# Attention with mixed heads and a token/channel MLP: another order in the last double steps and the tail

## The chip, the cores and the metric

The kernel runs on one core of one Trainium2 chip. The metric is the device time of one execution in microseconds (us), the median of the runs; it begins and ends a little outside the span from the first to the last instruction that the profile shows.

## The reference

```python
def _attn_ref(q, k, v, w_pre, w_post):          # q, k, v: (4, 12, 448, 64)
    scores = scale * np.matmul(q, k.transpose(0, 1, 3, 2))
    scores = np.einsum('bhij,hg->bgij', scores, w_pre)      # mixes the 12 heads
    scores = scores - np.max(scores, axis=-1, keepdims=True)
    attn = np.exp(scores)
    attn = attn / (np.sum(attn, axis=-1, keepdims=True) + 1e-09)
    attn = np.einsum('bhij,hg->bgij', attn, w_post)         # mixes them again
    return np.matmul(attn, v)

def _moe_ref(x, w_tok1, w_tok2, w_ch1, w_ch2):  # x: (4, 448, 768), the heads side by side
    h = np.maximum(x.transpose(0, 2, 1) @ w_tok1, 0.0) @ w_tok2
    u = x + h.transpose(0, 2, 1)
    return u + np.maximum(u @ w_ch1, 0.0) @ w_ch2
```

The four MLP weights arrive as 64-bit floats; the kernel converts each into a pair of single-precision parts, a high one and a remainder.

## The kernel before, in words

The attention part cuts each batch's 448 rows into four tiles (T = 0 to 15 over the batches), and each tile into groups of ten rows. One or two groups make a step (92 of them), two steps a double step J (46, from J = 0 to 45, with two more to fill the pipe). The order of all work is written out by hand; each engine takes its instructions in that order, and a planner at the start hands the score products (`qk`) and value products (`av`) of the tiles to the double steps. From J = 40 on there are no score products left, and each double step has one value product, of tile 13 (J = 40 to 42) or 14 (J = 43 to 45). Tile 15's three come behind the loop. "av(14,1)" is tile 14's second value product.

A step passes through three double steps. In the first (steps `na` and `nb`), `pre` mixes heads on TensorE (L169), `mx` takes two row maxima on VectorE (L177), `ex` takes the exponentials on ScalarE (L186), the first half at once for `na`. In the second (`ea`, `eb`), the rest of the exponentials follow, `rec` forms sums and reciprocals on VectorE (L195, L198), and GpSimd normalises (L200, L203). In the third (`pa`, `pb`), `post` mixes heads again on TensorE (L212) and `turn` transposes 32x32 blocks on VectorE (L225). `av` multiplies with v (L242); ScalarE copies one half of its result (L254), VectorE adds the other ("the sum", L256), and a DMA stores it (L257).

PSUM has two pools in this part. `pre` has two tiles. Another pair is shared by post, av and the score products, in turn: in J = 43 to 45 each of them needs the tile of the one before the last, and so waits for that one's `turn` or sum.

`cv_tick` moves the conversion of the weights on by one position i: a DMA loads unit i+5 (L356), ScalarE writes the high part of unit i (L377), VectorE assembles unit i+1 in three operations (L386, L390, L396), another engine forms the remainder of unit i (L394), GpSimd clamps magnitudes of unit i+2 (`cv_clamp`, L368), and ScalarE takes magnitudes of unit i+3 (`cv_abs`, L362). Units 0 to 7 are the token weights (128x256 four times, 128x224 four times), the others the channel weights. It is called 2, 1, 1, 3 times in the last four double steps, and 4 times among tile 15's value products.

`load_x` brings a batch's x back from DRAM (L345; batches 0 and 1 at the beginning of J = 43 and 44). `tr(b, hfs)` transposes halves of it on TensorE (L513: four PSUM tiles of three transpositions per half), ScalarE writes high parts (L518), VectorE remainders (L520). Then, for each batch, `tok1` and `tok2` multiply with the token weights (L528 to L530, L542, L543), with `tr` of the next batch in between; `tok2` also forms u (L559) and, for batch 0, its high part (L563) and remainder (`u_lo`, L580). `ch1` and `ch2` (from 442 us to the end) multiply with the channel weights. The tail before was in this order:

```python
    av(NT - 1, 0)
    tr(0, (0,))
    cv_tick(1)
    av(NT - 1, 1)
    tr(0, (1,))
    cv_tick(1)
    av(NT - 1, 2)
    cv_tick(2)
```

Of the kernel before, what the change touches and what calls it, by code (L numbers as in the profile page):

```python
# [14 lines left out]
ALU = mybir.AluOpType  # L15
AX = mybir.AxisListType
PSUM = bass.MemoryType.PSUM
# [19 lines left out]
def attn_mixer_kernel(  # L37
# [12 lines left out]
    nc = tc.nc  # L50
    f32 = lambda ap: ap.bitcast(F32)
# [11 lines left out]
    def en(name, **kw):  # L63
        p = tc.alloc_tile_pool(name=name, reuse_waits="tile", **kw)
        opens[name] = p
        return p

    def close(*names):
        for n in names:
            opens.pop(n).release()  # L70
# [233 lines left out]
    G = 0  # L304
# [60 lines left out]
    def cv_clamp(i):  # L365
        P = units[i][1]
        g = mags[i]
        nc.gpsimd.tensor_scalar(  # L368
            out=g[:P], in0=g[:P], scalar1=MAG_MIN, scalar2=MAG_MAX, op0=ALU.max, op1=ALU.min,
        )  # L370

# [79 lines left out]
    def step(i):  # L451
        return steps[i] if 0 <= i < NS else []

    for J in range(-2, ND):
        pa, pb, ea, eb, na, nb = [step(2 * J + i) for i in range(6)]
        if J == ND - 4:
            close("early")
            open_prep()
        if J == ND - 1:
            close("ps")  # L460
            a2 = en("a2", bufs=2, side="right")
            pst = en("pst", bufs=4, space=PSUM, side="right")
        for fn, *a in loads[J]:
            fn(*a)
        if J in (ND - 3, ND - 2):
            load_x(J - ND + 3)
        for st in (pa, pb):
            if st:
                post(st)
        if ea:  # L470
            ex(ea, 1)
        if pa:
            turn(pa)
        if ea:
            rec(ea)
            ex(eb, 0)
            ex(eb, 1)
        if pb:
            turn(pb)
        if eb:  # L480
            rec(eb)
        if J >= ND - 4:
            cv_tick((2, 1, 1, 3)[J - ND])
        if na:
            pre(na)
            mx(na)
        for a in value[J][:1]:
            av(*a)
        for a in score[J][:1]:
            qk(*a)  # L490
        if nb:
            pre(nb)
            ex(na, 0)
        for a in value[J][1:]:
            av(*a)
        for a in score[J][1:]:
            qk(*a)
        if nb:
            mx(nb)
        for st in (step(2 * J + 8), step(2 * J + 9)):  # L500
            for G in st:
                regroup(G)

    XN, H1 = {}, {}

    def tr(b, hfs=(0, 1)):
        x = XR[b]
        xn = XN.get(b) or [a2.tile([128, JT - i, DM], F32R, tag=f"xn{i}", bufs=1, name=f"xn{i}") for i in range(2)]
        for hf in hfs:
            for j in range(JT):  # L510
                p = pst.tile([128, 512], F32, tag="tr", name="tr")
                for d in range(3):
                    nc.tensor.transpose(  # L513
                        out=p[:, 128 * d:128 * d + 128], in_=x[hf][:, d, min(128 * j, 320):min(128 * j, 320) + 128],
                        identity=prep["ident"],
                    )
                cs = slice(384 * hf, 384 * hf + 384)
                nc.scalar.copy(out=xn[0][:, j, cs], in_=p[:, :384])  # L518
                lo_t, r = (xn[1][:, j, cs], 0) if j < 3 else (xn[0][:64, 3, cs], 64)
                nc.vector.tensor_tensor(out=lo_t, in0=p[r:, :384], in1=f32(xn[0])[r:, j, cs], op=ALU.subtract)  # L520
        XN[b] = xn

    def relu_split(p, h, l):
        nc.scalar.activation(out=h, in_=p, func=ACTF.Relu)  # L524
# [7 lines left out]
    def tok1(b):  # L532
        xn = XN.pop(b)
        h1 = [a3.tile([128, 2, DM], F32R, tag=f"h1{i}", bufs=1, name=f"h1{i}") for i in range(2)]
        for hf in range(2):
            for m in range(2):
                p = psa.tile([128, 512], F32, tag="t", bufs=4, name="pt1")
                cs = slice(384 * hf, 384 * hf + 384)
                w = [y[:, :, 128 * m:128 * m + 128] for y in prep["t1"]]
                for j in range(3):  # L540
                    mm3(p[:, :384], [y[:, j] for y in w], [y[:, j, cs] for y in xn], j == 0, False)
                nc.tensor.matmul(out=p[:, :384], lhsT=w[0][:, 3], rhs=xn[0][:, 3, cs], start=False, stop=False)  # L542
                nc.tensor.matmul(out=p[:, :384], lhsT=w[1][64:, 3], rhs=xn[0][64:, 3, cs], start=False, stop=True)  # L543
                relu_split(p[:, :384], h1[0][:, m, cs], h1[1][:, m, cs])
                if hf * 2 + m < 2:
                    cv_tick(1)
        H1[b] = h1

# [28 lines left out]
        return U[b, d][0]  # L577

    def u_lo(b, d, u):
        nc.vector.tensor_tensor(out=U[b, d][1], in0=u, in1=f32(U[b, d][0]), op=ALU.subtract)  # L580

    av(NT - 1, 0)
    tr(0, (0,))
    cv_tick(1)
    av(NT - 1, 1)
    tr(0, (1,))
    cv_tick(1)
    av(NT - 1, 2)
    cv_tick(2)
    close("mid", "late", "atp", "ps_w")  # L590
    psa = en("psa", bufs=2, space=PSUM)
    prep["w"] = en("wres", bufs=1)
# [101 lines left out]
```

## Time and profile before

| | us |
|---|---|
| median of 3 runs (797.56 to 800.02) | 798.28 |
| the profiled execution | 798.18 |
| its span, first to last instruction | 796.1 |
| TensorE busy (matmuls) | 765.5 |
| VectorE busy | 462.3 |
| ScalarE busy | 334.1 |
| GpSimd busy | 305.3 |

PE is TensorE's matmuls, PEld its weight loads, DVE is VectorE, ACT ScalarE, POOL GpSimd, SP the SyncE queue that issues the DMAs. Busy shares are means over stages with different limits; idle time of an engine matters where another waits for it. In the timelines a row has the start, the busy time, engine, line, operation, output and input, and in brackets the idle time of the engine ahead of it with what ended it.

### The profile page before, as it was taken

Reading aid. Unit: us, or ns where it says so; the run is one execution under the profiler, and the core shown is the slowest. Engines: PE = TensorE matmul, PEld = TensorE weight load, DVE = VectorE, ACT = ScalarE, POOL = GpSimd, SP = SyncE. Lnnn points to the kernel's source line nnn. Section 1 sums busy time; section 2 is a strip of 40 time slices with the busy share of each in tenths; the row PEclk is TensorE's granted clock in tenths of the full one; section 3 lists DMA queues with packets and bytes.
Section 4 is the critical chain, followed back from the end, with each engine's and each line's share of the span. In section 5 each row is a group of like instructions: output and inputs, shape, how many; then the busy total and the mean of one; then the engine's idle time right before and its main releaser. Section 6 shows DMA issues by size and latency. Waiting matters only on the chain.

```text
span 796.1 us, 21930 instructions
## 1 busy us (share of the span) xinstructions
PE 765.5 (96%) x9211; PEld 578.4 (73%) x9211; DVE 462.3 (58%) x822; ACT 334.1 (42%) x757; POOL 305.3 (38%) x292
## 2 busy tenths in 40 slices
PE   7879999999999999979999999999999999999998
PEld 3336555555555545557888999999999999999997
DVE  5766677777777677889899999950003100040002
ACT  3655766677766666556544355420001000020000
POOL 3663566555665465675267867600000000000000
PEclk9998999999999999999999999999999999999999
DMA  5784647755775474574565755351000300010001
GB/s 169 224 205 152 160 162 235 215 139 179 234 216 138 158 223 148 142 244 132 178 239 172 225 169 169 119 208 70 0 1 19 121 1 0 1 70 1 0 1 70
DMA packets 62594, 105.66 MB, mean 133 GB/s; under 512 B 20979, under 2 KB 49184, under 8 KB 61984
## 3 DMA queue, kind: packets, MB, share of 16 engines
q1 hardware_dynamic: 62080, 103.35, 42.1%
q8 instruction: 73, 1.20, 0.6%
q10 hardware_dynamic: 320, 0.87, 0.4%
q14 instruction: 25, 0.20, 0.1%
q0 software_dynamic: 96, 0.03, 0.0%
HBM read 49.18 MB, written 16.52 MB: 83 GB/s over the span
## 4 chain that ended last, share of the span: by engine, by line
PE 82%; DMA 7%; DVE 3%; ACT 2%; POOL 2%; issue 2%; SPq 1%; DVEq 0%; POOLq 0%; ACTq 0%
PE post L212 9%; PE pre L169 8%; PE av L242 7%; PE pc L528 7%; PE pc L529 7%; PE pc L530 7%; PE po L528 7%; PE po L530 7%; PE po L529 7%; PE qk L141 7%; DMA r<-s 4%; PE pt L528 2%; PE pt L530 2%; PE pt L529 2%; POOL e L203 1%
## 5 line engine op out<-in xcount | busy, mean ns | idle before, releaser
L203 POOL TENSOR_TENSOR e<-e,sm 128x896 f32<-128x896 f32 (+1 forms) x92 | 154.7, 1681 | 7.2
L525 DVE SCALAR_TENSOR_TENSOR rl<-pc,rh 128x448 fp32r<-128x448 f32 x48 | 29.8, 621 | 218.1 <-ACT rh L524 218.1
L225 DVE STREAM_TRANSPOSE at<-post 128x1024 f32<-128x1024 f32 (+1 forms) x92 | 111.9, 1216 | 40.7 <-PE post L212 40.6
L524 ACT ACTIVATE rh<-pc 128x448 fp32r<-128x448 f32 x48 | 26.1, 543 | 232.4 <-PE pc L530 232.3
L186 ACT ACTIVATE e<-pre,sm 128x448 f32<-128x448 f32 (+1 forms) x184 | 115.2, 636 | 8.3 <-DVE sm L177 8.0
L177 DVE TENSOR_REDUCE sm<-pre 128x2 f32<-128x896 f32 (+1 forms) x92 | 99.3, 1081 | 21.7 <-PE pre L169 21.3
L212 PE MATMUL post<-e,kpost 64*32 64x256 f32 x2880 | 99.3, 381 | 11.5 <-POOL e L203 4.4
L169 PE MATMUL pre<-r,kpre 64*64 64x448 f32 (+1 forms) x720 | 101.1, 554 | 7.5 <-DMA r<-s 4.4
L530 PE MATMUL pc<-u,w 128*128 128x448 f32 x288 | 105.2, 365 | 0.0
L529 PE MATMUL po<-rl,w 128*128 128x448 f32 x288 | 105.2, 365 | 0.0
L529 PE MATMUL pc<-u,w 128*128 128x448 f32 x288 | 105.2, 365 | 0.0
L528 PE MATMUL po<-rh,w 128*128 128x448 f32 x288 | 105.2, 365 | 0.0
L528 PE MATMUL pc<-u,w 128*128 128x448 f32 x288 | 105.2, 365 | 0.0
L530 PE MATMUL po<-rh,w 128*128 128x448 f32 x288 | 105.2, 365 | 0.0
L212 PEld LDWEIGHTS post<-e,kpost 64*32 64x32 f32 x2880 | 49.5, 106 | 70.8 <-issue 38.6
L141 PE MATMUL qk<-k,q 64*64 64x448 f32 (+2 forms) x768 | 97.7, 547 | 1.1 <-DMA k<-in_k_dram 0.5
L242 PEld LDWEIGHTS av<-at,v 64*64 64x64 f32 x2688 | 78.6, 136 | 23.3 <-DVE sm L195 9.8
L368 POOL TENSOR_SCALAR cv_g<-cv_g 128x384 f32<-128x384 f32 (+2 forms) x56 | 87.1, 1558 | 18.3 <-ACT cv_g L362 18.3
L200 POOL TENSOR_TENSOR e<-e,sm 128x128 f32<-128x128 f32 (+1 forms) x92 | 36.9, 401 | 143.2 <-ACT e L186 86.6
L242 PE MATMUL av<-at,v 64*64 64x120 f32 (+1 forms) x2688 | 84.3, 267 | 2.6 <-DVE x L256 2.5
L148 ACT COPY s<-qk 120x896 f32<-120x896 f32 (+1 forms) x84 | 75.5, 907 | 17.4 <-PE qk L141 11.1
L169 PEld LDWEIGHTS pre<-r,kpre 64*64 64x64 f32 (+1 forms) x720 | 33.3, 133 | 44.2 <-issue 31.9
(72 smaller groups left out, 1005.3 us busy)
## 6 DMA issues: line engine op xcount, KB each, us to landing
r<-s SPq DMA_DIRECT2D x176, 210.0 KB
cv_r<-in_w_ch_dram SPq DMA_DIRECT2D x48, 384.0 KB
v<-in_v_dram SPq DMA_DIRECT2D x16, 384.0 KB
xr<-x_dr SPq DMA_DIRECT2D x8, 672.0 KB
u_dr<-u SPq DMA_DIRECT2D x24, 224.0 KB
ur<-u_dr SPq DMA_DIRECT2D x4, 1344.0 KB
out_dram<-ur SPq DMA_DIRECT2D x24, 224.0 KB
k<-in_k_dram SPq DMA_DIRECT2D x21, 224.0 KB
```

What stands on the lines that cost most here:

```text
L141: nc.tensor.matmul(out=p[c:c + m, s, :S], lhsT=Q[T][r, h, c:c + m], rhs=K[b][r, h, :], start=True, stop=True)
L169: nc.tensor.matmul(out=p[64 * s:64 * s + 64, x, :S], lhsT=kpre[k], rhs=rt[a % NR][k], start=True, stop=True)
L177: nc.vector.tensor_reduce(out=s[:m, 0:2], in_=PP[st[0]][:m, :, :S], axis=AX.X, op=ALU.max, negate=True)
L186: nc.scalar.activation(out=E[st[0]][:m, x, :S], in_=p[:m, x, :S], func=ACTF.Exp, bias=s[:m, x:x + 1], scale=1.0, accum_out=s[:m, 2 + 2 * x ...
L203: nc.gpsimd.tensor_tensor(out=e[:m, :, :S], in0=e[:m, :, :S], in1=w.to_broadcast([m, 2, S]), op=ALU.mult)
L212: nc.tensor.matmul(out=p[32 * a:32 * a + 32, s, 256 * hf:256 * hf + 256], lhsT=kpost[k, 32 * hf:32 * hf + 32], rhs=ek[k, :, :, a, :], star ...
L225: nc.vector.transpose(out=AT[T][:, c:c + w].rearrange("p c f -> p (c f)"), in_=p[:, :w].rearrange("p c f -> p (c f)"))
L242: nc.tensor.matmul(out=p[64 * s:64 * s + 64, r, 10 * w * u:10 * w * (u + 1)], lhsT=V[b][k, 6 * u + h, j, :], rhs=at_[k, u, :w, :, f:f + 5] ...
L368: nc.gpsimd.tensor_scalar(out=g[:P], in0=g[:P], scalar1=MAG_MIN, scalar2=MAG_MAX, op0=ALU.max, op1=ALU.min,)
L528: nc.tensor.matmul(out=p, lhsT=a[0], rhs=x[0], start=first, stop=False)
L529: nc.tensor.matmul(out=p, lhsT=a[0], rhs=x[1], start=False, stop=False)
L530: nc.tensor.matmul(out=p, lhsT=a[1], rhs=x[0], start=False, stop=last)
```

## The change

In double steps without score products both `pre` come first, the second maximum stands right behind the first, and the value product follows. In J = 44 both `rec` stand ahead of their `turn`. At the end of J = 44 the PSUM pool of `pre` is closed (before, at the beginning of J = 45) and the first half of batch 0's x is transposed there. `cv_tick` moves from the middle of the last four double steps to their end, 2, 1, 2, 1 times; behind the loop it follows each of tile 15's value products and the transposition of the second half; and `tok1` of batch 0 calls it three times rather than two. The clamps of the token weights go from GpSimd to VectorE, and the remainders of batch 0's u from VectorE to GpSimd. The function `tr` itself only moves up in the file.

```diff
@@ cv_clamp @@
-        nc.gpsimd.tensor_scalar(
+        (nc.vector if i < 8 else nc.gpsimd).tensor_scalar(
             out=g[:P], in0=g[:P], scalar1=MAG_MIN, scalar2=MAG_MAX, op0=ALU.max, op1=ALU.min,
         )
@@ the loop over double steps @@
     for J in range(-2, ND):
         pa, pb, ea, eb, na, nb = [step(2 * J + i) for i in range(6)]
...
-        if J == ND - 1:
-            close("ps")
-            a2 = en("a2", bufs=2, side="right")
-            pst = en("pst", bufs=4, space=PSUM, side="right")
...
+        last = J == ND - 2
         if ea:
             ex(ea, 1)
+        if last:
+            rec(ea)
         if pa:
             turn(pa)
         if ea:
-            rec(ea)
+            if not last:
+                rec(ea)
             ex(eb, 0)
             ex(eb, 1)
+        if last:
+            rec(eb)
         if pb:
             turn(pb)
-        if eb:
+        if eb and not last:
             rec(eb)
-        if J >= ND - 4:
-            cv_tick((2, 1, 1, 3)[J - ND])
         if na:
             pre(na)
             mx(na)
-        for a in value[J][:1]:
+        lone = not score[J] and na
+        for a in value[J][:0 if lone else 1]:
             av(*a)
         for a in score[J][:1]:
             qk(*a)
         if nb:
             pre(nb)
             ex(na, 0)
-        for a in value[J][1:]:
+        if lone:
+            mx(nb)
+        for a in value[J][0 if lone else 1:]:
             av(*a)
         for a in score[J][1:]:
             qk(*a)
-        if nb:
+        if nb and not lone:
             mx(nb)
...
+        if J == ND - 2:
+            close("ps")
+            a2 = en("a2", bufs=2, side="right")
+            pst = en("pst", bufs=4, space=PSUM, side="right")
+            tr(0, (0,))
+        if J >= ND - 4:
+            cv_tick((2, 1, 2, 1)[J - ND])
@@ tok1 @@
-                if hf * 2 + m < 2:
+                if hf * 2 + m < (2 if b else 3):
                     cv_tick(1)
@@ u_lo and the tail @@
-        nc.vector.tensor_tensor(out=U[b, d][1], in0=u, in1=f32(U[b, d][0]), op=ALU.subtract)
-
-    av(NT - 1, 0)
-    tr(0, (0,))
-    cv_tick(1)
-    av(NT - 1, 1)
+        eng = nc.vector if b else nc.gpsimd
+        eng.tensor_tensor(out=U[b, d][1], in0=u, in1=f32(U[b, d][0]), op=ALU.subtract)
+
+    for hp in range(3):
+        av(NT - 1, hp)
+        cv_tick(1)
     tr(0, (1,))
     cv_tick(1)
-    av(NT - 1, 2)
-    cv_tick(2)
     close("mid", "late", "atp", "ps_w")
```

## Rows read from the trace of the kernel before

**Rows 1.** Busy time by stretch: stretch, us, each engine's busy us, PEclk, DMA share, GB/s

```profile
319.17:342.49 23.32, 22.14 (x545) 12.50 (x541) 20.37 (x36) 13.41 (x38) 15.23 (x18) 1.00 0.57 152
...
377.54:417.00 39.46, 38.59 (x203) 32.83 (x202) 36.41 (x62) 19.59 (x42) 18.37 (x14) 1.00 0.61 210
```

**Rows 2.** The chain of waits from 318 to 378: start, us, what

```profile
349.18 6.40 DMA cv_r<-in_w_tok_dram
...
357.33 0.99 DVE x L256 x3
```

**Rows 3.** TensorE in order of time: start, busy us, operation, idle before and what ended it

```profile
56.88 1.06 PE L169 MATMUL pre<-r,kpre 64*64 64x448 f32 x2 [2.74 <-DMA r<-s]
...
347.91 1.10 PE L212 MATMUL post<-e,kpost 64*32 64x256 f32 x32 [0.55 <-POOL e L203]
...
350.01 1.07 PE L212 MATMUL post<-e,kpost 64*32 64x256 f32 x16 [1.00 <-POOL e L203]
351.01 2.96 PE L242 MATMUL av<-at,v 64*64 64x120 f32 x112
...
357.95 2.37 PE L242 MATMUL av<-at,v 64*64 64x90 f32 x54 [2.52 <-DVE x L256]
...
375.72 2.07 PE L513 MATMUL tr<-ident,xr 128*128 128x128 f32 x12 [1.17 <-DVE xn L520]
```

**Rows 4.** Busy time by stretch, the two with a low granted clock

```profile
57.55:64.38 6.83, 6.12 (x72) 4.36 (x75) 1.53 (x2) 0.58 (x1) 1.51 (x1) 0.50 0.72 222
357.93:361.34 3.41, 3.39 (x61) 3.19 (x62) 3.28 (x9) 1.48 (x6) 1.65 (x2) 0.50 0.46 125
```

**Rows 5.** VectorE in order of time

```profile
348.00 0.59 DVE L256 TENSOR_TENSOR x<-av,x 128x240 f32<-128x240 f32 x1 [0.74 <-ACT x L254]
349.11 1.25 DVE L225 STREAM_TRANSPOSE at<-post 128x1024 f32<-128x1024 f32 x1 [0.52 <-PE post L212]
351.15 0.72 DVE L225 STREAM_TRANSPOSE at<-post 128x512 f32<-128x512 f32 x1 [0.79 <-PE post L212]
351.79 0.41 DVE L386 TENSOR_SCALAR cv_g<-cv_g 128x256 uint32<-128x256 uint32 x1
352.23 0.43 DVE L390 SCALAR_TENSOR_TENSOR cv_a<-cv_r,cv_g 128x256 uint32<-128x256 uint32 x1
352.69 0.42 DVE L396 SCALAR_TENSOR_TENSOR cv_a<-cv_r,cv_a 128x256 uint32<-128x256 uint32 x1
353.03 0.29 DVE L386 TENSOR_SCALAR cv_g<-cv_g 128x256 uint32<-128x256 uint32 x1
...
353.81 0.83 DVE L396 SCALAR_TENSOR_TENSOR cv_a<-cv_r,cv_a 128x256 uint32<-128x256 uint32 x1
355.60 0.81 DVE L386 TENSOR_SCALAR cv_g<-cv_g 128x256 uint32<-128x256 uint32 x1 [0.96 <-POOL cv_g L368]
...
358.24 2.06 DVE L520 TENSOR_TENSOR xn<-tr,xn 128x384 fp32r<-128x384 f32 x4
...
367.75 0.28 DVE L386 TENSOR_SCALAR cv_g<-cv_g 128x224 uint32<-128x224 uint32 x1 [0.37 <-POOL cv_g L368]
...
369.96 0.74 DVE L390 SCALAR_TENSOR_TENSOR cv_a<-cv_r,cv_g 128x224 uint32<-128x224 uint32 x1
...
375.12 4.17 DVE L520 TENSOR_TENSOR xn<-tr,xn 128x384 fp32r<-128x384 f32 x8
```

**Rows 6.** ScalarE in order of time

```profile
343.20 0.63 ACT L186 ACTIVATE e<-pre,sm 128x448 f32<-128x448 f32 x1
...
349.30 0.43 ACT L362 ACTIVATE cv_g<-cv_r 128x256 f32<-128x256 f32 x1 [1.33 <-DMA cv_r<-in_w_tok_dram]
```

**Rows 7.** GpSimd in order of time

```profile
349.94 2.10 POOL L368 TENSOR_SCALAR cv_g<-cv_g 128x256 f32<-128x256 f32 x2
...
388.38 1.01 POOL L394 TENSOR_TENSOR w<-cv_a,w 128x384 fp32r<-128x384 f32 x1 [14.13 <-ACT w L377]
```

**Rows 8.** SyncE's queue in order of time

```profile
340.65 0.82 SPq L345 DMA_DIRECT2D xr<-x_dr  x2
```

More of the change, by code (lines that the diff above doesn't have):

```diff
@@ L452, in step @@
         return steps[i] if 0 <= i < NS else []
[L454 to L458, printed above, removed]
-        if J == ND - 1:
-            close("ps")
-            a2 = en("a2", bufs=2, side="right")
-            pst = en("pst", bufs=4, space=PSUM, side="right")
[L463 to L474, printed above, removed]
-            rec(ea)
[L476 to L479, printed above, removed]
-        if eb:
-            rec(eb)
-        if J >= ND - 4:
-            cv_tick((2, 1, 1, 3)[J - ND])
-        if na:
-            pre(na)
-            mx(na)
-        for a in value[J][:1]:
-            av(*a)
-        for a in score[J][:1]:
-            qk(*a)
-        if nb:
-            pre(nb)
-            ex(na, 0)
-        for a in value[J][1:]:
[L495 to L502, printed above, removed]
     XN, H1 = {}, {}
@@ L521, in tr @@
         XN[b] = xn
+    for J in range(-2, ND):
+        pa, pb, ea, eb, na, nb = [step(2 * J + i) for i in range(6)]
+        if J == ND - 4:
+            close("early")
+            open_prep()
+        for fn, *a in loads[J]:
+            fn(*a)
+        if J in (ND - 3, ND - 2):
+            load_x(J - ND + 3)
+        for st in (pa, pb):
+            if st:
+                post(st)
+        last = J == ND - 2
+        if ea:
+            ex(ea, 1)
+        if last:
+            rec(ea)
+        if pa:
+            turn(pa)
+        if ea:
+            if not last:
+                rec(ea)
+            ex(eb, 0)
+            ex(eb, 1)
+        if last:
+            rec(eb)
+        if pb:
+            turn(pb)
+        if eb and not last:
+            rec(eb)
+        if na:
+            pre(na)
+            mx(na)
+        lone = not score[J] and na
+        for a in value[J][:0 if lone else 1]:
+            av(*a)
+        for a in score[J][:1]:
+            qk(*a)
+        if nb:
+            pre(nb)
+            ex(na, 0)
+        if lone:
+            mx(nb)
+        for a in value[J][0 if lone else 1:]:
+            av(*a)
+        for a in score[J][1:]:
+            qk(*a)
+        if nb and not lone:
+            mx(nb)
+        for st in (step(2 * J + 8), step(2 * J + 9)):
+            for G in st:
+                regroup(G)
+        if J == ND - 2:
[5 more added lines that the diff above has]
+            cv_tick((2, 1, 2, 1)[J - ND])
     def relu_split(p, h, l):
```

## The prediction

> **What bounds the kernel now.** The table of times ahead gives 798.18 us for the profiled execution, 2.08 of them around its span of 796.1, and a median of 798.28, 0.10 above it. All sums below are made against 798.18. A difference under 0.3% (2.4 us) is what a measurement of this kernel can't tell from no change. I read the trace from the whole to the place.
>
> The busy time by stretch [rows 1] splits the part that the diff touches. From 377.54 to 417.00 TensorE is busy 38.59 of 39.46 us. The four double steps without scores (J = 40 to 43, 319.17 to 342.49) have TensorE at 22.14 of 23.32 and VectorE at 20.37. Between the two, TensorE has its holes, and the chain of waits [rows 2] walks through just that place: a load of the conversion's raw weights (6.40 us from issue to landing), then the sums of the last attention tiles on VectorE (0.99).
>
> TensorE's own rows [rows 3] give the holes: 0.55 and 1.00 before the two last post products (GpSimd's normalisation), 2.52 before av(15,1), 1.17 before the fifth transposition of batch 1. The 2.52 cost more than itself: right behind it the granted clock was 0.50, the 1.2 GHz level, for 3.41 us, and the one other fall inside the kernel, of 6.83 us, follows a hole of 2.74 [rows 3, 4]; behind the holes of 1.17 and less TensorE ran on at 2.4 GHz.
>
> What the reader is to see in VectorE's rows [rows 5]: from 357.33, where the held sums start [rows 2], to 375.12, where batch 1's remainders start, it is hardly ever idle; the longest wait is 0.37, for a clamp on GpSimd. So the place where TensorE next stands still (375.72, for VectorE [rows 3]) is set by how much VectorE has to have done by then, and by when it can start on it. This is the bound on which I build.
>
> **The change, part by part.** *Both pre first (J = 40 to 43).* Before, VectorE's second maximum stands behind the attention sum, which waits for ScalarE's copy. After, the maximum runs while the copy is made. But the copy now stands behind an exponential on ScalarE (0.63) [rows 6], the value product starts one pre later, and the second post product of the next double step needs the PSUM pair that this sum frees. Walking the queues with such durations I find the last sum of J = 43 ending at 344.1, and J = 44's second post product starting there, some 0.4 early. The stretch has only 23.32 − 22.14 = 1.18 us of TensorE idle [rows 1], so the ends are −1.2 and, if each of the four later value products is paid with 0.2, +0.8; I take −0.4.
>
> *J = 44: reciprocals ahead of transpositions.* ScalarE's abs(0), ahead of the copy before, now stands at the end of J = 43, and ex(ea,1) begins near 343.8 instead of 343.20 [rows 6]. rec(ea) waits for it, and turn(pa) now waits for rec(ea): it runs from 344.9 to 346.1. That frees the PSUM pair of av(14,1), which so loses the 0.4 again and starts at 346.1. GpSimd gets its last two normalisations some 0.7 earlier.
>
> *tr(0,0) at the end of J = 44.* Its twelve transpositions (1.5 us) follow av(14,1) at 347.6 and so cover the holes of 0.55 and 1.00; the posts then start at 349.1 and 350.1, against 347.91 and 350.01 [rows 3]. Its x must be there: issued at 340.65 [rows 8], and with the 6.40 us that a load of this stretch took [rows 2] it lands near 347.1. That leaves half a microsecond of cover; if x lands later, TensorE waits in front of both posts, for up to 1 us.
>
> *Conversion behind each value product.* This is where the price arises. At the end of J = 44 VectorE now has, ahead of J = 45's turn(pa): the sum of av(14,1), until 349.1; four remainders of tr(0,0), 2.06; a clamp; a conversion step of three operations, 1.24 (from 351.79 to 353.03); another clamp [rows 5]. A clamp on VectorE isn't in the trace. Below it lies the shift-and-mask with two constants on the same tile, 0.29, and 0.32 with the gap behind it [rows 5]; above it GpSimd's own pace, 1.05 (2.10 for two) [rows 7]; I take 0.30, since the form, size and engine are those of the first. So turn(pa) runs from 353.0 to 354.2, where it began at 349.11 [rows 5]. av(14,2) needs the PSUM pair that it frees: it starts at 354.27 instead of 351.01 [rows 3], behind a hole from 351.2 that is 3.07 us long. In exchange nothing of the 2.52 before av(15,1) is left, since the abs that waits for its load (1.33 once) [rows 6] now stands behind the copy.
>
> Does the clock fall in that hole? Both holes of over 2.5 us were followed by a fall, so I take a fall as somewhat likelier than not. At 2.4 GHz the sum of av(14,2) ends at 357.3. At 1.2 the product takes 2.92 instead of 1.46 and the sum ends at 358.9. Before, it ended near 357.9: it is the first half of the 0.99 that starts at 357.33 [rows 2].
>
> What VectorE still owes from there until batch 1's remainders: before, both sets of four remainders of batch 0, and conversion steps 3 to 8. After, one set, steps 1 to 8, and six clamps. That is two steps more, 2 × 1.24 = +2.48; one set less, −2.06; six clamps, 6 × 0.30 = +1.80; and the wait of 0.37 for GpSimd's clamp goes [rows 5]. Sum: +1.85. With the sum of av(14,2) ending 1.0 later (clock down) this is +2.8, with 0.6 earlier (clock up) +1.2. Each clamp that costs 1.05 instead would add 0.75.
>
> *Behind that.* Batch 0's six u remainders go to GpSimd. TensorE has 0.87 idle in that whole stretch [rows 1], so taking them off VectorE is worth 0, and at most 0.87. On GpSimd they need some 6 × 1.2 = 7.1 us (1.01 for 384 columns, times 448/384), inside a pause of 14.13 [rows 7]; without that cover the conversions of tok1(1) would come later, for which nothing on TensorE waits. The third conversion in tok1(0) is the one that the tail gave up: no work is added.
>
> *The second hole.* TensorE comes to batch 1's fifth transposition at about the time it did, so the 1.17 there becomes 2.4 to 4.0. A fall of the clock behind it costs half of 3.41, 1.7, in a stretch that is full.
>
> A rule of the Trainium skill bears on the moved clamps. In the rows a conversion operation took 0.83 and another 0.81 while GpSimd was at work, against 0.42 and 0.29 elsewhere [rows 5]. The Trainium skill (SBUF — State Buffer, Who interferes with whom) says that VectorE's second port pair is also GpSimd's, that whoever starts first has it for a whole instruction, and that the other is fully blocked. By that rule, clamps that leave GpSimd also shorten VectorE's other operations; I leave these at their old mean, and the rule's full effect is part of the third rival.
>
> **The rivals.** *No fall: +1.2, 799.4.* The same bound, both holes at 2.4 GHz. For it: 3.07 is near 2.52, and my estimate may be off by half a microsecond. *Both fall: 2.8 + 1.7 = +4.5, 802.7.* For it: the second hole is as long as the first. It decides whether VectorE comes more than some 1.5 late to batch 1's remainders.
>
> *VectorE is set free: faster.* Its waits of 0.74, 0.52, 0.79 and 0.96 between 347 and 356 are filled with conversion work (3.0), the wait of 0.37 goes, and the five operations that were slowed between 353.81 and 369.96 return to their short times: 0.41 and 0.52 for the two named, 0.3 each for the three others (the last 0.74 against 0.43) [rows 5], 1.8. Against that stand eight clamps, 2.4. That is −2.8, 795.4; TensorE could follow, with 2.52 and 1.17 of holes and 1.7 lost to the clock. It decides whether VectorE reaches J = 45's turn(pa) before 351. Against it: VectorE takes its work in order, and 3.9 us of it stand ahead.
>
> *Nothing moves: 798.2.* The new hole is as long as the old ones (3.07 for 2.52 + 0.55), the clock falls once as before, and the clamps vanish in waits.
>
> **How the numbers follow.** Forecast: VectorE's bound, and one of the two falls: 798.18 + 2.8 = 801.0, chance 0.35, own range 799.9 to 802.0. No fall 0.17, both falls 0.18, VectorE set free 0.15, nothing 0.15. The range 795.6 to 803.2 reaches to all of them and leaves out the outer parts of both falls and of VectorE set free. Slower by over 0.3% (above 800.7): 0.23 of the forecast, 0.17 of both falls, 0.02 of no fall, together 0.42. Faster: 0.13 of VectorE set free and 0.02 of nothing, 0.15. Within 0.3%: the remaining 0.43.
>
> **What would show it.** In the trace after: J = 45's turn(pa) right behind a clamp on VectorE near 353; a hole of about 3 us on TensorE before av(14,2), and none over 1 before av(15,1); a granted clock of 0.50 behind that hole or behind the one in batch 1's transpositions; the first of batch 1's remainders near 378 instead of 375.12; two maxima back to back in J = 40 to 43, and that stretch within 1 us of 23.32. I am wrong if VectorE reaches J = 45's turn(pa) without a hole on TensorE, if clamps there cost much over 0.3, if tr(0,0) waits over a microsecond for its x, or if TensorE and not VectorE sets the time of batch 1's fifth transposition.

## The result, and the profile of the changed kernel

| | before | changed |
|---|---|---|
| median, us (lowest to highest, runs) | 798.31 (797.56 to 800.02, 4) | 808.65 (805.67 to 812.19, 4) |
| profiled execution, us | 798.18 | 809.97 |
| its span, us | 796.1 | 807.8 |

The changed kernel is slower: the ratio is 1.0121, with a 95% interval of 1.0080 to 1.0163. The prediction was 801.0 in a range of 795.6 to 803.2, so the result lies above all of it.

The spans differ by 11.7 us, and they divide into two parts. The channel stage (`ch1`, `ch2`) begins at 447.05 instead of 442.18, which is 4.87; and it takes 356.85 instead of 350.01, which is 6.84. The first part is the one the prediction is about. The second it does not have at all.

**The first part** lies where the prediction put it. TensorE in order of time, changed kernel (columns as in [rows 3]):

```profile
347.40 1.81 PE L242 MATMUL av<-at,v 64*64 64x120 f32 x56 [0.63 <-DVE sm L195]
...
350.60 1.95 PE L212 MATMUL post<-e,kpost 64*32 64x256 f32 x48
355.64 5.64 PE L242 MATMUL av<-at,v 64*64 64x120 f32 x168 [3.10 <-DVE at L225]
362.00 1.40 PE L242 MATMUL av<-at,v 64*64 64x90 f32 x56 [0.71 <-ACT cv_g L362]
...
379.39 2.63 PE L463 MATMUL tr<-ident,xr 128*128 128x128 f32 x12 [3.49 <-DVE xn L470]
```

The two posts of J = 45 run without the holes of 0.55 and 1.00 of [rows 3], and the 2.52 ahead of av(15,1) is gone. In their place stand a hole of 3.10 ahead of av(14,2), ended by `turn`, and a short one of 0.63 ahead of av(14,1), ended by a `rec`; and the 1.17 in batch 1's transpositions has become 3.49.

Busy time by stretch of the changed kernel (columns as in [rows 1]): the four double steps without scores, the two stretches behind those holes, and the channel stage.

```profile
319.20:344.17 24.97, 22.52 (x545) 13.14 (x541) 21.14 (x36) 12.58 (x38) 16.17 (x19) 1.00 0.54 145
...
356.03:359.44 3.41, 3.41 (x86) 3.41 (x82) 0.45 (x2) 0.91 (x3) 0.03 (x1) 0.50 0.09 28
379.92:383.33 3.41, 3.41 (x15) 3.24 (x15) 3.05 (x6) 1.92 (x4) 0.00 (x0) 0.50 0.00 0
...
447.05:803.90 356.85, 356.85 (x1728) 324.06 (x1727) 122.44 (x223) 65.12 (x131) 54.51 (x34) 1.00 0.20 64
```

The granted clock was 0.50 behind both holes. The four double steps took 24.97, against 23.32 in [rows 1], with as many matmuls: TensorE idled 2.45 instead of 1.18 and was counted busy for 22.52 instead of 22.14, where the prediction had a gain.

VectorE in order of time, changed kernel (columns as in [rows 5]):

```profile
350.49 2.06 DVE L470 TENSOR_TENSOR xn<-tr,xn 128x384 fp32r<-128x384 f32 x4
352.56 0.29 DVE L368 TENSOR_SCALAR cv_g<-cv_g 128x256 f32<-128x256 f32 x1
352.89 0.29 DVE L386 TENSOR_SCALAR cv_g<-cv_g 128x256 uint32<-128x256 uint32 x1
353.22 0.42 DVE L390 SCALAR_TENSOR_TENSOR cv_a<-cv_r,cv_g 128x256 uint32<-128x256 uint32 x1
353.68 0.42 DVE L396 SCALAR_TENSOR_TENSOR cv_a<-cv_r,cv_a 128x256 uint32<-128x256 uint32 x1
354.02 0.29 DVE L368 TENSOR_SCALAR cv_g<-cv_g 128x256 f32<-128x256 f32 x1
354.34 1.85 DVE L225 STREAM_TRANSPOSE at<-post 128x1024 f32<-128x1024 f32 x2
359.15 0.60 DVE L256 TENSOR_TENSOR x<-av,x 128x240 f32<-128x240 f32 x1 [2.96 <-ACT x L254]
...
378.80 4.33 DVE L470 TENSOR_TENSOR xn<-tr,xn 128x384 fp32r<-128x384 f32 x8
```

The posts had ended at 352.55. `turn` waits until 354.34, because four remainders, a clamp, a conversion step and a second clamp stand ahead of it: the queue of the prediction, operation by operation. A clamp took 0.29. Then VectorE, with its conversion work still to do, stands still for 2.96, while av(14,2) runs at half the clock.

**The second part** is spread evenly over 1728 matmuls. The same stage before:

```profile
442.18:792.19 350.01, 350.01 (x1728) 324.42 (x1727) 121.85 (x223) 64.90 (x131) 54.47 (x34) 1.00 0.20 64
```

The order, the count and the granted clock are the same, and TensorE is busy without a break in both. But a matmul follows the one before it after 350.01 / 1727 = 202.7 ns before and 356.85 / 1727 = 206.6 ns after. I call these the short and the long step.

### The profile page after: what moved, and what is told of

It is laid out like the page before. It is cut to its first block, busy times and chain, and to the rows that moved or that the text cites. A ratio compares the mean times of both kernels' runs of the same rounds, so it can differ in the third digit from the quotient of the medians.

```text
span 807.8 us, 21928 instructions
## 1 busy us (share of the span) xinstructions
PE 772.7 (96%) x9211; PEld 579.5 (72%) x9211; DVE 460.8 (57%) x824; ACT 333.1 (41%) x757; POOL 304.0 (38%) x290
## 4 chain that ended last, share of the span: by engine, by line
PE 52%; DVE 1%; ACT 0%; issue 0%
PE pc L539 7%; PE pc L541 7%; PE pc L540 7%; PE po L541 7%; PE po L539 7%; PE po L540 7%; PE pt L539 2%; PE pt L540 2%; PE pt L541 2%; PE tr L463 1%; PE pt L554 1%; DVE ur L641 0%; PE pt L553 0%; DVE h L536 0%; DVE xn L470 0%; DVE cv_a L390 0%
## 5 line engine op out<-in xcount | busy, mean ns | idle before, releaser
L169 PE MATMUL pre<-r,kpre 64*64 64x448 f32 (+1 forms) x720 | 98.6, 550 | 5.1 <-DMA r<-s 2.5
L368 POOL TENSOR_SCALAR cv_g<-cv_g 128x384 f32<-128x384 f32 x48 | 78.5, 1637 | 18.3 <-ACT cv_g L362 18.3
```

The source lines that it names most:

```text
L169: nc.tensor.matmul(out=p[64 * s:64 * s + 64, x, :S], lhsT=kpre[k], rhs=rt[a % NR][k], start=True, stop=True)
L368: (nc.vector if i < 8 else nc.gpsimd).tensor_scalar(out=g[:P], in0=g[:P], scalar1=MAG_MIN, scalar2=MAG_MAX, op0=ALU.max, op1=ALU.min,)
```

## The experiments

Two theories for the first part, one for each step of the sum. **Queue**: the two long holes, and the clock behind them, are VectorE's conversion work ahead of `turn` and of batch 1's remainders. **Ring**: both `pre` first costs time rather than saving it. The rival to both: VectorE is not what TensorE waits for up to tok2. For the channel stage there are three more, **Entry**, **Program** and **Chance**, which the first expectation below explains. Besides the times, each run is read by where TensorE begins things, counted from its last score product, since the work ahead of that is alike in all kernels ("last post" is the last of the post matmuls, and the length runs from the first to the last matmul's start):

| kernel | last post | tok2 | channel stage | length of that stage |
|---|---|---|---|---|
| before | 32.00 | 58.84 | 123.48 | 350.01 |
| changed | 33.43 | 62.94 | 128.32 | 356.85 |
| changed, again | 34.23 | 64.44 | 130.74 | 350.07 |
| changed, third time | 33.52 | 63.67 | 129.96 | 350.07 |
| changed, last sum early | 34.31 | 62.90 | 129.15 | 356.91 |
| changed, calls behind turns | 33.49 | 60.64 | 126.68 | 350.06 |
| the same, and unit 8 later | 34.20 | 59.49 | 125.05 | 357.71 |
| changed, value product between | 31.97 | 62.13 | 127.18 | 356.90 |
| the three together | 31.66 | 56.93 | 122.47 | 350.01 |
| before, both pre first | 33.90 | 60.83 | 125.48 | 350.01 |
| before, clamps on VectorE | 32.06 | 59.95 | 124.65 | 350.06 |
| before, u remainders on GpSimd | 32.35 | 59.22 | 123.85 | 350.01 |
| before, last sum late | 32.00 | 58.85 | 123.49 | 350.32 |

### The channel stage: what sets its step?

In the changed kernel's first profile the step switched from the short to the long one at the second product of the stage. TensorE there, with its weight loads (PEld):

```profile
450.50 0.37 PE L541 MATMUL pc<-u,w 128*128 128x448 f32 x1
450.60 0.19 PEld L539 LDWEIGHTS pc<-u,w 128*128 128x128 f32 x1
450.70 0.38 PE L539 MATMUL pc<-u,w 128*128 128x448 f32 x1
450.71 0.19 PEld L540 LDWEIGHTS pc<-u,w 128*128 128x128 f32 x1
```

A load otherwise starts within 0.01 of the matmul ahead; this one came 0.10 behind it, when VectorE's last u sum had ended. Hence the theory Entry. The changed kernel, unaltered:

> The changed kernel, unaltered. In its first profile the 1728 matmuls of the channel stage follow each other every 206.7 ns instead of 202.7 (before), 6.84 us in sum, from the second product on, whose first weight load was held for some 0.09 us by VectorE's last u sum. Theory Entry (the hold sets the step, and it comes from the order of the work): 206.7 ns again, 808 to 810 us. Theory Program (something else in the changed program sets it): the same. Theory Chance (each execution takes one of the two steps at random): 202.7 about as often as 206.7, so the times fall into two groups near 803 and 810.

It took 803.98 (ratio 1.0060, 1.0036 to 1.0083). Its channel stage had the short step from the second product on:

```profile
447.92:797.99 350.07, 350.07 (x1728) 324.63 (x1727) 122.01 (x223) 64.94 (x131) 54.59 (x34) 1.00 0.20 65
```

So one and the same program has both steps. Program has fallen, and the 6.84 are no price of the edit in every execution.

The changed kernel with the last u sum earlier:

```diff
-            if b and d % 2 == 0:
+            if b and d % 2 == 0 and (b, d) != (B - 1, KD - 2):
                 cv_tick(1)
```

> The changed kernel without the conversion step that stands ahead of VectorE's last u sum (it is made up for right behind it). Theory Entry: the last sum ends over 0.5 us earlier, the second product's first weight load is not held, the stream keeps its 202.7 ns to the end, the channel stage takes 350.0 us instead of 356.9, and the time is 802 to 804. Theory Program: 206.7 ns and 808 to 810 as before. Theory Chance: either.

The sum now ended 2.2 us ahead of that load, nothing was held, and yet the stage had the long step from its first product on (356.91). The median of its 4 executions is 812.63, not the 802 to 804 of theory Entry (803.44 to 815.25; ratio 1.0150, 1.0075 to 1.0225). Two of them took 815, some 5 us more than the profiled one with its long step (810.34); nothing here explains these 5 us.

The kernel before with the last sum late:

```diff
+            if (b, d) == (B - 1, KD - 1):
+                nc.vector.tensor_copy(out=u, in_=x[d // 3][:, d % 3, :])
             nc.vector.tensor_tensor(out=u, in0=p[:, :S], in1=x[d // 3][:, d % 3, :], op=ALU.add)
```

> The kernel before, with one copy of 128x448 on VectorE ahead of the last u sum (a price of 0.3 to 0.6 us on VectorE, off TensorE's path but for the hold). Theory Entry: the sum ends at or after 445.8 instead of 445.49, the weight load of the second product is held for 0.1 to 0.5 us, the step becomes 206.7 ns, and the time rises by 7 to 805. Theory Program: the hold itself, at most 0.5, so 798.3 to 798.8, and 202.7 ns. Theory Chance: either step.

```profile
445.87 0.36 PE L530 MATMUL pc<-u,w 128*128 128x448 f32 x1
446.14 0.91 DVE L386 TENSOR_SCALAR cv_g<-cv_g 128x384 uint32<-128x384 uint32 x1
446.28 0.19 PEld L528 LDWEIGHTS pc<-u,w 128*128 128x128 f32 x1 [0.42 <-DVE u L561]
```

Here the load was held for 0.41, and the step stayed short (350.32, the hold included; the time is 799.12, ratio 0.9994, 0.9958 to 1.0030). A hold does not make the long step, and without one it can come: Entry as it was stated has fallen too. Chance was left, but as what: drawn once for an execution, or at each start of the stream? For that the kernel before, made to stop 48 times:

```diff
-            if c:
-                ch2(b, c - 1)
+            if c < NC - 1:
+                ch2(b, c)
```

> The kernel before, with each second channel product directly behind its first one, so that TensorE has to wait for the relu 48 times (some 1.3 us each, +60 us, near 860). Each product then begins from a standing engine. The unaltered kernels showed that the step of the channel stage (202.7 or 206.7 ns) changes from execution to execution of one program. If it is drawn each time the stream starts anew, this profile shows both steps among its 48 pairs of products; if it is a state of the whole execution, all 48 have the same; if each product has its own fixed one by its buffers, the same pattern repeats in each of the four batches.

It took 866.18 in its one execution. A pair is a first product (18 matmuls) and the second product behind it, which has to wait; the next pair follows without a stop. First products of two successive pairs, the first and the last of their 18 matmuls:

```profile
530.22 0.36 PE L528 MATMUL pc<-u,w 128*128 128x448 f32 x1
...
533.66 0.36 PE L530 MATMUL pc<-u,w 128*128 128x448 f32 x1
...
539.78 0.37 PE L528 MATMUL pc<-u,w 128*128 128x448 f32 x1
...
543.29 0.37 PE L530 MATMUL pc<-u,w 128*128 128x448 f32 x1
```

Seventeen steps took 3.44 in the one and 3.51 in the other. Of the 48 streams that set out from such a stop, 43 settled at the short step and 4 at the long one, in no order that repeats by batch; the first of the 48 ran for the most part at a granted clock of 0.50 and counts in neither. The long step was kept into the next pair's first product. So the step is drawn anew at a start, and kept until the stream is held again; and since both stand in one execution, it is no state of the program, of the execution or of the chip. Other runs agree. In "unit 8 later" (below) the stream ran with the short step until the end of batch 0 (a hold of 1.60 early in it changed nothing), was held there, and came out with the long one:

```profile
532.43 0.36 PE L544 MATMUL po<-rh,w 128*128 128x448 f32 x1
532.73 0.47 PE L542 MATMUL pc<-u,w 128*128 128x448 f32 x1
533.39 0.47 PE L543 MATMUL pc<-u,w 128*128 128x448 f32 x1 [0.19 <-DVE u L597]
```

In the five profiles in which the second product's load was not held at all (before, both pre first, u remainders on GpSimd, last sum early, unit 8 later) the stream went on there as it had entered, short four times and long once. In the eight in which that load did wait for the last u sum, the step changed there in five, four times from long to short and once the other way, and stayed in three.

The changed kernel a third time, with more executions:

> The changed kernel, unaltered, for how its executions spread. By its own edits (theory Queue and theory Ring) it takes 803 to 805 where the channel stage keeps the short step and 810 to 812 where it keeps the long one; the kernel before 797 to 800 and 804 to 807. If the long step is drawn as often in both kernels, the two medians differ by 4 to 5 us; if the changed kernel draws it more often, by more.

It took 803.83 in the median of 12 (801.64 to 808.22; ratio 1.0049, 1.0023 to 1.0076), its profiled execution again with the short step. None of the sixteen executions of these two runs reached 810, and their times don't fall into two groups, as theory Chance had expected. By the ratios the changed kernel is 4 to 5 us slower than the one before in these runs; the prediction's steps have to explain about that much. In the two profiles themselves the channel stage began 7.26 and 6.48 later than before (first profile: 4.84). The difference lies at the second hole: the granted clock was low there for 6.83 in both, twice the 3.41 of the first profile. In the second run of the changed kernel (columns as in [rows 1]):

```profile
378.36:385.19 6.83, 6.05 (x22) 5.66 (x23) 5.07 (x10) 2.31 (x6) 0.36 (x1) 0.50 0.01 3
```

**What stays open** is whether the changed kernel draws the long step more often. Of the eight profiles of the changed kernel and its variants, three had it for all but at most the first product, and one for the greater part of the stage; of the five of the kernel before and its variants (without the one with breaks), none beyond the first product. Such counts don't decide it. Nor is it known which of the other three executions behind the 808.65 had it.

### The tail: Queue

J = 44's conversion calls moved behind J = 45's turns, nothing else:

```diff
+        if J == ND - 1:
+            cv_tick(2)
         lone = not score[J] and na
...
-            cv_tick((2, 1, 2, 1)[J - ND])
+            cv_tick((2, 1, 0, 1)[J - ND])
```

> The changed kernel with the two conversion calls of J = 44 moved behind both turns of J = 45, ahead of av(14,2). Theory Queue (the 3.10 us hole is VectorE's 1.75 us of conversion ahead of turn(pa), and the clock falls for it): turn(pa) begins at 352.6 instead of 354.3, the hole shrinks to some 1.3, no fall behind it, av(14,2)'s sum ends near 356.8 instead of 359.7, and tok2 begins near 379.0 instead of 381.7. Rival (the clock falls there whatever the hole): a fall of 3.4 remains, and tok2 begins near 380.0. Rival (VectorE is not the bound up to tok2): tok2 begins at 381.5 or later. Channel stage, theory Entry: its step stays 206.7 ns only if the last u sum stays as late against TensorE as it was (3.50 us behind the first channel product); the order from tok1 on is not touched, so I expect 206.7.

```profile
351.56 2.94 PE L242 MATMUL av<-at,v 64*64 64x120 f32 x112 [1.35 <-DVE at L225]
...
374.50 2.82 PE L463 MATMUL tr<-ident,xr 128*128 128x128 f32 x12 [3.47 <-DVE xn L470]
```

The hole shrank from 3.10 to 1.35, the clock stayed at 1.00 behind it, and tok2 began 2.3 us earlier (60.64 instead of 62.94; I had expected 2.7). The second hole, which the edit does not touch, stayed at 3.47, with its fall, which lasted 6.83. The profiled execution took 799.16 with the short step, where I had expected the long one; the median of 8 is 803.4 (ratio 1.0051, 1.0014 to 1.0089), which can't be told from the unaltered changed kernel's 803.83. Queue holds for the first hole, by the profile.

For the second hole, the three VectorE operations on the first channel unit taken out of tok1(0) as well:

```diff
-            cv_step(i, eng)
+            cv_step(i, eng, 2 if i == 7 else 3)
...
-                if hf * 2 + m < (2 if b else 3):
+                if hf * 2 + m < 2:
                     cv_tick(1)
+                if b == 0 and hf * 2 + m == 2:
+                    cv_step(7, nc.gpsimd, 1)
```

(With 1, `cv_step` writes only unit 7's own parts; with 2, it assembles only the next unit.)

> The changed kernel with the two conversion calls of J = 44 behind J = 45's turns (as in the run before), and also without the three VectorE operations on the first channel unit (0.35 + 0.90 + 0.74) ahead of batch 1's remainders; they come with the next call, in tok1(1). Theory Queue: the second hole shrinks from 3.47 to 1.4, the clock does not fall behind it, tok2 begins 58.6 us behind the last score product (60.6 in the run before, 62.9 in the changed kernel, 58.8 before) and the channel stage 123.2 behind it (126.7, 128.3, 123.5). With the short step of the channel stage 795.5 to 797, with the long one 802.5 to 804. Rival (VectorE is not what the second hole waits for): 60.6 and 126.7 stay, 799.

```profile
375.52 2.47 PE L464 MATMUL tr<-ident,xr 128*128 128x128 f32 x12 [1.94 <-DVE xn L471]
```

The hole shrank by 1.53 to 1.94, not to the 1.4 that I had expected, and the clock still fell behind it. tok2 began 1.15 earlier, and the channel stage paid 1.8 back: every later call came one position later, and a product waited 1.60 for VectorE's remainder of the relu, which stood behind conversion work there. Queue holds in kind; the size was missed. The time, 805.71 (ratio 1.0057, 1.0022 to 1.0093), is no better; the profiled execution also drew the long step for the greater part of the channel stage, and of the other nine it isn't known.

The clamps alone, on the kernel before:

```diff
-        nc.gpsimd.tensor_scalar(
+        (nc.vector if i < 8 else nc.gpsimd).tensor_scalar(
```

> The kernel before with the eight clamps of the token weights on VectorE, nothing else. By the prediction's terms: +8 x 0.29 on VectorE, its waits for GpSimd's clamps (0.96, 0.37, 0.31) go, so batch 1's remainders come at most 0.7 later and tok2 begins 58.8 to 59.5 us behind the last score product (58.8 before). By the rival in which VectorE is set free of GpSimd's neighbourhood, operations that took 0.7 to 0.8 take 0.4: tok2 begins at 57.5 or earlier.

tok2 began 1.11 later (59.95, outside the 58.8 to 59.5 that I had expected), and the time is the same (799.79; ratio 1.0002, 0.9968 to 1.0036). "VectorE set free" has no support in it. The price shows elsewhere than expected: a new hole of 1.59 in tok1(0), ended by VectorE's attention sum, and the clock fell behind that hole instead of behind the 2.63 ahead of av(15,1).

The u remainders alone:

```diff
-        nc.vector.tensor_tensor(out=U[b, d][1], in0=u, in1=f32(U[b, d][0]), op=ALU.subtract)
+        (nc.vector if b else nc.gpsimd).tensor_tensor(out=U[b, d][1], in0=u, in1=f32(U[b, d][0]), op=ALU.subtract)
```

> The kernel before with batch 0's six u remainders on GpSimd, nothing else. The prediction gave 0 for it, at most 0.87 of gain. From tok2's begin to the channel stage: 64.65 us before, 63.8 to 64.7 here. Rival (GpSimd's remainders slow VectorE's u sums beside them, and tok1(1) with them): over 64.9.

From tok2 to the channel stage it took 64.63, against 64.65 (ratio 0.9999, 0.9973 to 1.0025). The 0 of the prediction is right.

### The double steps without scores: Ring

Both `pre` first on the kernel before, nothing else:

```diff
-        for a in value[J][:1]:
+        lone = not score[J] and na
+        for a in value[J][:0 if lone else 1]:
             av(*a)
...
+        if lone:
+            mx(nb)
-        for a in value[J][1:]:
+        for a in value[J][0 if lone else 1:]:
...
-        if nb:
+        if nb and not lone:
             mx(nb)
```

> The kernel before with both pre first in J = 40 to 43, nothing else. The prediction took -0.4 with ends -1.2 and +0.8 for it: the last post of the loop begins 31.6 us behind the last score product instead of 32.0 (ends 30.8 and 32.8), and tok2 moves by the same or less. Rival (the copy behind an exponential and the later value product cost more than the second maximum gains): 32.2 to 32.8.

The four double steps took

```profile
319.75:344.71 24.96, 22.86 (x544) 13.41 (x540) 21.15 (x36) 13.01 (x39) 16.14 (x19) 1.00 0.55 148
```

against 23.32 in [rows 1], and the last post began 1.90 later. The rival was right, and beyond its upper end. By the starts of their posts J = 40 and 41 take 11.56 in the changed kernel, whose rows are alike (before: 11.53); the loss is in J = 42 and 43. TensorE, ScalarE and VectorE there:

```profile
335.44 0.60 PE L169 MATMUL pre<-r,kpre 64*64 64x448 f32 x3 [0.38 <-DMA r<-s]
335.44 0.14 PEld L169 LDWEIGHTS pre<-r,kpre 64*64 64x64 f32 x3 [1.16 <-DMA r<-s]
...
338.01 0.60 ACT L254 COPY x<-av 128x240 f32<-128x240 f32 x1 [1.09 <-PE av L242]
...
338.65 0.58 DVE L256 TENSOR_TENSOR x<-av,x 128x240 f32<-128x240 f32 x1 [1.08 <-ACT x L254]
...
339.37 1.10 PE L212 MATMUL post<-e,kpost 64*32 64x256 f32 x32 [0.39 <-DVE x L256]
```

Without the value product ahead of it, the second `pre` of J = 42 comes to its rows before their DMA has landed. From there on it goes round: the value product behind it is later, ScalarE's copy waits 1.09 for that, VectorE's sum waits 1.08 for the copy (not for the maxima, which were done), and the second post of the next double step waits for that sum's PSUM pair.

The rows themselves also come later. SyncE's queue holds the store of J = 40's sum (L257) ahead of the loads of J = 42's rows (L161). Before, and then in the changed kernel:

```profile
325.21 0.56 SPq L257 DMA_DIRECT2D x_dr<-x  x1
325.86 4.12 SPq L161 DMA_DIRECT2D r<-s  x4
```

```profile
326.37 0.56 SPq L257 DMA_DIRECT2D x_dr<-x  x1
327.02 4.13 SPq L161 DMA_DIRECT2D r<-s  x4
```

The later value product and the exponential ahead of its copy make the sum later, the store waits for the sum, and the loads behind the store are issued 1.16 later; TensorE's weight load then waited 1.16 for these rows. No run takes the store out of their way, so how the loss divides between this and the missing cover is not shown. This part moved tok2 by 1.99; the time is 802.01 (ratio 1.0029, 0.9993 to 1.0064), which is not told from no change.

The other way round, the changed kernel without this part:

```diff
-        lone = not score[J] and na
+        lone = False
```

> The changed kernel without the first part: in J = 40 to 43 the value product stands again between the two pre. Theory Ring (both pre first costs the four double steps 1.64 us, as the run with that part alone showed, since the second post waits for the attention sum, which stands behind both maxima): the last post begins 31.8 to 32.0 us behind the last score product instead of 33.4 to 34.2, tok2 61.3 to 61.5 behind it instead of 62.9, and the time is 1.6 lower. Rival (VectorE's work sets tok2 whatever comes ahead): the second hole grows by 1.6 and tok2 stays at 62.9.

```profile
321.29:344.61 23.32, 22.15 (x545) 12.49 (x541) 20.40 (x36) 12.97 (x37) 15.23 (x18) 1.00 0.56 148
...
380.49 1.76 PE L463 MATMUL tr<-ident,xr 128*128 128x128 f32 x7 [3.47 <-DVE xn L470]
```

The four double steps are back at 23.32, the last post at 31.97. The second hole is as long as before (3.47), so VectorE's work moved along with TensorE's, and the gain reached the channel stage: 127.18, against 128.32 in the first profile of the changed kernel, whose low stretch there was as long. At tok2 itself only 0.81 of the expected 1.6 shows, partly because more of the low clock here lay in front of tok2 (2.65 of the 3.41, against 1.76). The time is 803.4 (ratio 1.0043, 1.0004 to 1.0082), not told from the changed kernel's 803.83; the profiled execution had the long step. Ring holds by the profile.

### The three together

The changed kernel with the value product between the two `pre`, J = 44's calls behind J = 45's turns, and the first channel unit out of tok1(0), but with one more call in tok2(0), so that later weights keep their places:

```diff
-            if b and d % 2 == 0:
+            if (d % 2 == 0) if b else d == 3:
                 cv_tick(1)
```

> The changed kernel with three things undone or moved: the value product between the two pre in J = 40 to 43, J = 44's conversion calls behind J = 45's turns, and the first channel unit's VectorE operations out of tok1(0) into tok2(0) (one call there, so that the channel weights are not late). Theory Queue and theory Ring together: tok2 begins 57.0 us behind the last score product (62.9 changed, 58.8 before), the channel stage 121.7 to 123.4 behind it (128.3 and 123.5), the channel stage takes 350.0 or 356.9 by its step. Against the kernel before in like executions: 0 to 2 us faster. Rival (a new wait for the later weights, or a clock fall behind a hole of 1.3): 123.5 or later.

```profile
351.34 2.94 PE L242 MATMUL av<-at,v 64*64 64x120 f32 x112 [1.35 <-DVE at L225]
...
372.75 2.47 PE L464 MATMUL tr<-ident,xr 128*128 128x128 f32 x12 [1.94 <-DVE xn L471]
```

tok2 began at 56.93 and the channel stage at 122.47, both the earliest of all; that stage took 350.01. The profiled execution took 796.47, against 798.18 before. Over all executions the median is 799.49, against 800.15 (ratio 0.9991, 0.9958 to 1.0024): not distinguished from the kernel before, but what the changed kernel lost in the tail is gone. One fall is left there, behind the 1.94. No run tests J = 44's reciprocals or its early transposition alone.

## Why the prediction was wrong

The time lies 7.65 above the forecast. In the profiled execution three steps failed: a gain of 0.4 that was a loss of 1.65, one fall of the clock where there were two, and a channel stage without a term, which took 6.84 more. By the ratios of the two repeated runs alone, 802.2 to 803.1, the time would lie inside the range, near its upper end.

**Right: the queue on VectorE.** The hole ahead of av(14,2) was 3.10 (predicted 3.07), a clamp 0.27 to 0.29 (0.30), the `turn` stood right behind a clamp, and no hole over 1 was left ahead of av(15,1). From the end of av(14,2)'s sum (359.75) to batch 1's remainders (378.80) VectorE took 19.05, which is the 17.2 of before plus the 1.85 of the sum; that it agrees to the hundredth is luck, since a second wait for a clamp went as well (0.31 before, at 372.08), which the sum doesn't have. The second hole was 3.49, inside 2.4 to 4.0, but by two misses that cancel in part: the remainders began at 378.80 (forecast: near 378), and TensorE came to that place 1.4 later, not at about the time it did. The transpositions at the end of J = 44 covered both holes, x was there in time, and the u remainders cost nothing.

**Wrong in sign: "I take −0.4" for both pre first.** It was +1.65 in the four double steps, outside its ends of −1.2 and +0.8. The step walked ScalarE's and VectorE's queues, and left out what the second `pre` itself waits for: its rows' DMA, which the value product had covered, and SyncE's queue, in which that DMA stands behind the store of the sum. J = 43's last sum ended at 345.53, not 344.1, and `turn(pa)` began 1.3 later than forecast (354.34 for 353.0) for this reason: with the value product between, av(14,2) began 35.48 behind the last score product, where the forecast has 35.57 and the changed kernel 36.90.

**Wrong in size: one fall of the clock of two.** The forecast took one fall with 0.35 and both with 0.18, as if each were a toss. But both holes come from VectorE's backlog and are of one size: in all five profiles with the calls in front of `turn` (the changed kernel three times, last sum early, value product between), both holes measured 3.09 to 3.49, and the clock fell at both. "Both fall", 802.7 or +4.5, was the right case, but that its size is near the 4.84 of the first profile is luck in part: with both falls and the value product between, the channel stage began only 3.70 later than before (127.18 for 123.48), and the loss of both `pre` first, which the sum lacks, made up for that. Nor has a fall one price: behind the second hole the low clock lasted 3.41 in three of the five profiles and 6.83 in the two others.

**Missing: the step of the channel stage.** The prediction has no term for this stage: it put its change at nothing, without a reason. The long step costs 6.84, more than any term of the sum, and took the recorded profile from about 803 to 809.97. Nothing in a single profile of the kernel before shows the second value. The three executions of it then known spread over 2.5 us, and the prediction allowed 0.3% (2.4 us) for what a measurement can't tell; later executions of the same kernel lay between 796.1 and 807.7.

**The rule on the shared port.** The prediction left VectorE's slow operations at their old mean, though the clamps leave GpSimd. That was right, since GpSimd's remainders stay. VectorE and GpSimd side by side in the changed kernel:

```profile
362.14 0.78 DVE L390 SCALAR_TENSOR_TENSOR cv_a<-cv_r,cv_g 128x256 uint32<-128x256 uint32 x1
363.95 0.83 DVE L386 TENSOR_SCALAR cv_g<-cv_g 128x256 uint32<-128x256 uint32 x1
```

```profile
361.73 0.91 POOL L394 TENSOR_TENSOR t<-cv_a,t 128x256 fp32r<-128x256 f32 x1 [1.58 <-ACT t L377]
363.90 0.73 POOL L394 TENSOR_TENSOR t<-cv_a,t 128x256 fp32r<-128x256 f32 x1 [1.26 <-ACT t L377]
```

GpSimd's two remainders end at 362.64 and 364.63, and the VectorE operations that began inside them end at 362.92 and 364.78, 0.28 and 0.15 later; alone they take 0.42 and 0.29. The Trainium skill (SBUF — State Buffer, Who interferes with whom) says that the one who comes second to the shared pair of ports is blocked for the whole instruction of the other; the trace agrees in that neither ended before GpSimd's did, though both then needed 0.14 less than alone.

## What to carry to other kernels

An operation put "behind" another on one engine stands ahead of something else on it: count what is queued in front of the next transposition or copy that frees a PSUM tile, since that is where TensorE waits, and work which can wait belongs behind it. A matmul stream may also be covering a DMA; before moving it, look at what the instruction behind it waits for, and at what stands ahead of that DMA in its own queue. Two holes of one size that one engine's backlog makes had the same outcome in all five profiles here: don't price them as two tosses. And a stage without any waits still has its own spread from execution to execution: compare stages between profiles, counted from a common point, before a difference in the total is put down to an edit.

## What the runs showed of the hardware

**Two steps of one stream.** With a weight load for each matmul (128x128 weights, 448 columns, single precision as fp32r), the stream settles at a start either at 202.7 ns (steps of 198 to 207 in turn) or at a flat 206.7, at the same granted clock of 1.00, and in no profile did it change without a hold: up to 1728 matmuls in a row. In the kernel with breaks, by the start and end times of the trace, the first matmul that no longer waited began 18 ns behind the end of its weight load in the four long cases, and 11 to 15 ns behind it in the 43 short ones, so which one it becomes seems to hang on a few nanoseconds; that is a reading of one profile and was not tested by itself. How to make it the short one was not found. The Trainium skill (TensorE: Matmul & The Clock Gate, Back-to-back issue gap) gives, for an isolated matmul, a gap of the columns at 2.4 GHz plus 2.5 ns, by which 448 columns would be estimated at 189.2, and for a stream with a weight load for each matmul some 131 ns at 512 columns; both steps of this case are longer than either, and the measurements decide.

**The length of a hole alone does not tell whether the clock falls.** Behind holes of 1.35 to 1.36 ahead of av(14,2) it stayed at 1.00 in all three runs that had one; at 1.94 it fell both times, and at 3.09 to 3.49 in all eleven cases, for 3.41 or for 6.83. But with both pre first on the kernel before, it went to 0.50 right behind a hole of 1.00 (for 6.83), and with the clamps on VectorE it stayed at 1.00 behind one of 2.63 and fell at the 1.59 that came 8.5 us later.
